# One 3x512-column VectorE transpose per block in place of three of 512 columns

## The chip, the cores and the metric

The program runs on one core of a Trainium2 chip. The metric is the device time of one execution in microseconds (us), as the median of several runs; lower is better. TensorE is called PE here, its weight loads PEld, VectorE DVE, ScalarE ACT, GpSimd POOL and SyncE SP, as in the profile.

## The reference

Eight sequences of 4096 tokens with 192 channels pass through a causal convolution of 7 taps, whose taps are a softmax shared by the 24 channels of a head, and then through a two-layer MLP with SiLU, 192 to 2048 to 192, all in float32:

```python
w = softmax(weight)                                  # 8 heads x 7 taps
x_pad = concatenate([zeros((B, 6, D)), x], axis=1)
out[b, s, h, g] = sum_k w[h, k] * x_unf[b, s, k, h, g]
x = out.reshape(B * S, D)                            # 32768 x 192
h = x @ w_in                                         # 192 x 2048
g = h * (1.0 / (1.0 + np.exp(-h)))
return (g @ w_out).astype(np.float32)                # 2048 x 192
```

## The kernel before

**Tiling.** The 32768 tokens are cut into 32 blocks of 1024 (`NB`), each block into two halves of 512 (`TB`). The 192 channels are three groups of 64 (`NK` = 3). In a tile of 128 partitions, partitions 0 to 63 hold 64 channels of the first half and 64 to 127 the same channels of the second.

**The input of a block.** `load` (L172) brings group k of a block from DRAM to `nat[:, k]` with four DMAs on SP's queue, 32 tokens to a partition in the order that leaves each 32x32 square still to be turned. `turn_in` (L462) turns group k with one VectorE stream transpose from `nat[:, k]` into `xt[:, k, 6:518]` (recorded at L465); the first 6 columns of `xt` are the halo. There is one `xt` tile for all blocks (`xts[b] = xts[0]`). `halo_in` (L477) then fills the halo: POOL copies the last 6 columns of the block before, and an SP DMA takes those of the first half to the second. `conv` (L490) makes the convolution of group k tap by tap, from `xt` back into `nat`: tap 0 on ACT, taps 1 to 6 on DVE (L499). `spread` (L506) copies the result by SP DMAs to the tile `dup`, and `win` makes sums and differences of it, so that both row halves of PE can read their operands.

**The MLP.** The first product is made in a form with fewer multiplications: for each of five groups g (handled in the order 0, 4, 1, 2, 3) `product` (L611) makes fifteen products r of a 64-row weight with a 64-row operand, in one row half of PE each (r in 0, 1, 2, 4, 5, 6, 11, 14 in rows 64 to 127, the others in rows 0 to 63). They add up in PSUM banks along three chains, and `sums_h` (L662) takes partial values out between two steps of a chain: `u` copies one to SBUF (ACT), `X` and `a` add a second chain to it, `b` subtracts the third chain (all DVE, recorded at L668), and `S` applies SiLU (ACT). The third chain of every group lies in bank 4, and `X4` writes bank 6, onto which product 11 then accumulates. The second product (`out_slot`, L741) uses the whole array in four column tiles; before it, `sum_g` (L709) makes differences of the SiLU outputs on DVE.

**The order.** Nothing in the steady part is left to a scheduler: `PLAN` (L81) is a list of tokens for one period, written out by hand, and `step` (L858) carries them out in that order for b = 3 and on (L1075); `START` (L107) is a longer list for the first three blocks. A token has a name and digits: `P12.2` is product 12 of group 2, `u2.3` output 2 of group 3; `+` sends it to the next block, `-` and `=` to the one or two before. An engine gets its instructions in the order of the tokens and carries them out in that order. `i.k` calls `turn_in` for the block after. In `PLAN` the three stand well apart, and each has work of its engine behind it:

```text
P3.4 -M7.0 S2.0 +i.2 u2.4 | P0.0 | P7.0 X2.4 | ... a5.0 ...
P7.1 a0.4 | P0.1 +i.1 u5.3 sp.1 | P12.1 a5.1 | ... -o.0 | P4.1 u2.2 b1.1 | ...
P11.1 -o.3 u0.2 | P13.2 S1.1 a0.1 | P6.3 S4.1 | P9.2 +i.0 | P0.2 b5.1 u2.3 +ha.0
| P3.3 S0.0 X4.2 | P1.3 S2.2 | P12.2 u1.2 | P11.2 X2.3 | P7.2 u0.3 b1.2 | ...
```

`ha.0` is `halo_in`. The tap-0 step of group 2, `+v.20`, comes eleven slots after `+ha.0`, and that of group 1 three slots later.

In `START` the third of the three tokens is `-i.2` for block 2, `i.2` for block 3 and `+i.1` for block 4. Block 0 is turned group by group ahead of everything, and block 1 by `i.0`, `i.1`, `i.2` in one go before the list begins. From block 5 to block 31, 27 blocks, the third token is the `+i.0` of `PLAN`.

Of the kernel before, what the change touches and what calls it, by code (L numbers as in the profile page):

```python
# [17 lines left out]
def kernel(  # L18
# [33 lines left out]
    NK = D // R  # L52
    grp = D // H
    pad = K - 1
    TB = 512
# [99 lines left out]
    def pin(ins):  # L155
        return tc.keep_in_program_order(ins)
# [13 lines left out]
    nats, xts, gs = {}, {}, {}  # L170
# [288 lines left out]

    tails = {}  # L460

    def turn_in(b, k):  # L462
        xts[b] = xts[0]
        pin(
            nc.vector.transpose(  # L465
                xts[b][:, k, pad : pad + TB], nats[b][:, k, :, :].rearrange("p k c -> p (k c)")
            )
        )
        if not b and k == NK - 1:
            tail_of(b)  # L470

    def tail_of(b):
        if (b + 1) * TT % S:
            tails[b + 1] = xpool.tile([R, NK, pad], F32, tag="tail", name="tail", bufs=2)
            pin(nc.sync.dma_start(out=tails[b + 1], in_=xts[b][R:P, :, TB : TB + pad]))
# [382 lines left out]
    def step(b, token):  # L858
# [19 lines left out]
        elif name[0] in "uXabS":  # L878
            sums_h(b, name, *digits)
        elif name == "t":  # L880
            sum_g(b, *digits)
        elif name[0] == "D":
            i, (j, e) = int(name[1]), digits
            for half in range(2) if i == 3 and b == NB - 1 else (None,):
                out_slot(b, j, i, e, half)
        elif name[0] in "Mzyx":
            merge(b, name, *digits)
        elif name == "o":
            turn_out(b, *digits)
        elif name == "st":  # L890
            store_out(b, *digits)
        elif name == "dp":
            next(downs)
        elif name == "cp":
            copy_plain(b, *digits)
        elif name == "go":
            pool.tensor_copy(warm, nats[1][:, digits[0], 0, 0:1])
            for g in (2, 3):
                for e in range(2):
                    combine(g, e)  # L900
        elif name == "ld":
            if b + 1 < NB:
                load(b + 1, digits)
        elif b + 1 < NB:
            {"i": turn_in, "ha": halo_in, "v": conv, "sp": spread, "w": win}[name](
                b + 1, *digits[: 1 + (name == "v")]
            )
# [97 lines left out]
    def conv_pe(k):  # L1005
        by_pe[k] = [bank() for _ in range(2)]
        for i in range(K):
            for n in range(2):
# [8 lines left out]
                )  # L1017

    turn_in(0, 0)

    vec.memset(xts[0][R:P, 1:NK, 0:pad], 0.0)
# [4 lines left out]
    round_in(0, 0)  # L1026
    diagonal(1)
    turn_in(0, 1)
    conv_pe(1)
    for j in (1, 2):  # L1030
# [80 lines left out]
```

## Time and profile before

| what | value |
|---|---|
| median of 3 runs | 2349.09 us (2348.8 to 2349.61) |
| the profiled execution's own time | 2349.19 us |
| its span in the profile | 2347.5 us |
| busy PE / DVE / ACT | 2340.3 / 2099.6 / 1187.3 us |
| input transposes (L465) | 96, 66.8 us busy, 698 ns mean |
| steady period, from one `i.2` to the next | 72.14 us (1121.67 to 1193.81 us) |

The span is what the profile covers of the 2349.19 us; 1.7 us lie around it. Starts and durations in the timeline are in us; the end of a matmul is modelled, so that consecutive matmuls overlap in the records, and the distance from start to start tells more than the busy time. Each product of `PLAN` shows as two matmuls of 512 columns in one row half of PE, 0.43 us from start to start; the two row halves run side by side. A wait that a product has is carried by its weight load, which is in the PEld rows.

### The profile page before, as it was taken

Reading aid. Unit: us, or ns where it says so; the run is one execution under the profiler, and the core shown is the slowest. Engines: PE = TensorE matmul, PEld = TensorE weight load, DVE = VectorE, ACT = ScalarE, POOL = GpSimd, SP = SyncE. Lnnn points to the kernel's source line nnn. Section 1 sums busy time; section 2 is a strip of 40 time slices with the busy share of each in tenths; the row PEclk is TensorE's granted clock in tenths of the full one; section 3 lists DMA queues with packets and bytes.
Section 4 is the critical chain, followed back from the end, with each engine's and each line's share of the span. In section 5 each row is a group of like instructions: output and inputs, shape, how many; then the busy total and the mean of one; then the engine's idle time right before and its main releaser. Section 6 shows DMA issues by size and latency. Waiting matters only on the chain.

```text
span 2347.5 us, 43988 instructions
## 1 busy us (share of the span) xinstructions
PE 2340.3 (100%) x17630; PEld 1061.0 (45%) x17630; DVE 2099.6 (89%) x2877; ACT 1187.3 (51%) x2275; POOL 96.8 (4%) x168
## 2 busy tenths in 40 slices
PE   9999999999999999999999999999999999999998
PEld 4344444444444444434444444444444444444445
DVE  8899989899899998998998999989999989899876
ACT  4345644456544466444564445654446644456443
POOL 4920000000000000000000000000000000000000
PEclk9999999999999999999999999999999999999999
DMA  7232212222121221222221222212222212222111
GB/s 158 52 66 48 47 27 47 38 53 53 29 41 36 53 53 31 39 43 46 53 49 31 42 38 53 53 29 42 36 53 53 38 33 45 43 53 44 20 24 25
DMA packets 451245, 106.56 MB, mean 45 GB/s; under 512 B 423584, under 2 KB 428704, under 8 KB 451040
## 3 DMA queue, kind: packets, MB, share of 16 engines
q1 hardware_dynamic: 447392, 101.78, 23.7%
q8 instruction: 138, 2.26, 0.4%
q0 software_dynamic: 448, 1.58, 0.3%
q10 hardware_dynamic: 3200, 0.39, 0.1%
q14 instruction: 67, 0.55, 0.1%
HBM read 31.46 MB, written 25.17 MB: 24 GB/s over the span
## 4 chain that ended last, share of the span: by engine, by line
PE 99%; DVE 0%; ACT 0%; issue 0%; ACTq 0%
PE ps L741 47%; PE ps L625 42%; PE ps L642 5%; PE ps L762 2%; PE ps L571 2%; PE ps L1010 1%; PE ps L423 0%; DVE t L709 0%; ACT g L686 0%; DVE cmb L163 0%; ACT u L163 0%; DVE osb L163 0%; DVE osb L829 0%; DVE g L668 0%; PE ps L449 0%
## 5 line engine op out<-in xcount | busy, mean ns | idle before, releaser
L625 PE MATMUL ps<-win,wr 64*128 64x512 f32 x1550 | 720.3, 597 | 0.0
L741 PE MATMUL ps<-g,wo 128*32 128x512 f32 x2976 | 702.4, 593 | 0.0
L625 PE MATMUL ps<-win,ws 64*128 64x512 f32 x1550 | 631.3, 595 | 0.0
L741 PE MATMUL ps<-t,wo 128*32 128x512 f32 (+2 forms) x4528 | 545.7, 446 | 0.0
L674 ACT COPY u<-ps 128x512 f32<-128x512 f32 x775 | 446.8, 586 | 173.6 <-PE ps L625 161.4
L741 PE MATMUL ps<-t,wx 128*32 128x512 f32 x2976 | 495.5, 592 | 0.1
L625 PE MATMUL ps<-dup,wr 64*128 64x512 f32 x868 | 425.4, 593 | 0.0
L499 DVE SCALAR_TENSOR_TENSOR nat<-xt,taps,nat 128x512 f32<-128x512 f32 x564 | 411.3, 753 | 3.8 <-ACT nat L496 3.6
L686 ACT ACTIVATE g<-g 128x512 f32<-128x512 f32 x465 | 286.1, 633 | 231.5 <-DVE g L668 231.5
L804 ACT COPY yx<-ps 32x512 f32<-32x512 f32 x150 | 86.9, 579 | 574.0 <-PE ps L741 572.3
L709 DVE TENSOR_TENSOR t<-g 128x1024 f32<-128x1024 f32 x248 | 300.6, 1219 | 51.1 <-PE ps L741 43.4
L625 PEld LDWEIGHTS ps<-win,wr 64*128 64x128 f32 x1550 | 275.6, 186 | 150.4 <-issue 67.8
L668 DVE TENSOR_TENSOR g<-u,ps 128x512 f32<-128x512 f32 x465 | 311.2, 680 | 28.8 <-PE ps L625 14.6
L625 PE MATMUL ps<-dup,ws 64*128 64x512 f32 x682 | 324.2, 599 | 0.0
L709 DVE TENSOR_TENSOR t<-g,t 128x1024 f32<-128x1024 f32 x248 | 301.8, 1217 | 12.2 <-PE ps L741 9.4
L741 PEld LDWEIGHTS ps<-t,wo 128*32 128x32 f32 x4528 | 186.7, 110 | 274.1 <-issue 247.6
L625 PEld LDWEIGHTS ps<-win,ws 64*128 64x128 f32 x1550 | 254.7, 186 | 110.5 <-issue 40.8
L686 ACT ACTIVATE g<-ps 128x512 f32<-128x512 f32 x465 | 266.8, 597 | 41.1 <-PE ps L625 38.4
L668 DVE TENSOR_TENSOR ps<-u,ps 128x512 f32<-128x512 f32 x310 | 214.7, 692 | 43.7 <-ACT g L686 19.0
L741 PE MATMUL ps<-g,wx 128*32 128x512 f32 x1488 | 250.5, 592 | 0.0
L741 PEld LDWEIGHTS ps<-g,wo 128*32 128x32 f32 x2976 | 170.2, 110 | 120.9 <-issue 118.9
L741 PEld LDWEIGHTS ps<-t,wx 128*32 128x32 f32 x2976 | 120.5, 110 | 217.5 <-issue 202.3
(90 smaller groups left out, 1764.5 us busy)
## 6 DMA issues: line engine op xcount, KB each, us to landing
dup<-nat SPq DMA_DIRECT2D x345, 128.0 KB, 2.3
nat<-in_x_dram SPq DMA_DIRECT2D x382, 64.0 KB, 2.4
out_dram<-osb SPq DMA_DIRECT2D x376, 64.0 KB, 2.0
raw<-in_moe_w_out_dram SPq DMA_DIRECT2D x8, 384.0 KB, 3.6
raw<-in_moe_w_in_dram SPq DMA_DIRECT2D x12, 192.0 KB, 4.7
ws<-wr POOLq DMA_DIRECT2D x8, 192.0 KB, 5.0
raw<-in_moe_w_in_dram SPq DMA_DIRECT2D x6, 128.0 KB, 3.1
xt<-xt SPq DMA_DIRECT2D x31, 4.5 KB, 1.9
```

The source lines that it names most:

```text
L499: nc.vector.scalar_tensor_tensor(out=dst, in0=src, scalar=tap, in1=dst, op0=ALU.mult, op1=ALU.add)
L571: nc.tensor.matmul(hs[a, n, e], rows(wr[j], e)[:, a, k, :], rows(d, e)[:, n, k, :], start=k == 0, stop=k == NK - 1,)
L625: nc.tensor.matmul(to[:, cols], raw(g, *LEFT[e][r], e), rhs[:, cols], start=first, stop=True, skip_group_check=True,)
L642: nc.tensor.matmul(banks[PLAIN_BANKS[n and 1 + e]][:, cols], rows(wr[j] if own == e else ws[j], e)[:, a, k, :], rows(dups[b], e)[:, SLOT[e ...
L668: pin(nc.vector.tensor_tensor(out_, u, v, op=op))
L674: pin(nc.scalar.copy(us[b, g, o][:, cols], t1[:, cols]))
L686: pin(nc.scalar.activation(h, src, AF.Silu))
L709: pin(nc.vector.tensor_tensor(t[i // 2][:, i % 2, :], u, v, op=ALU.subtract))
L741: nc.tensor.matmul(accs[b][at][SQ * q : SQ * q + SQ, to], lhs[:, e, SQ * k : SQ * k + SQ], rhs[:, e, ts(q, TB // 4) if i == 5 else to], st ...
L762: nc.tensor.matmul(banks[DOWN_BANKS[k]][R * n : R * n + R, :], wo[j][:, a, e, R * k : R * k + R], gs[b, j, a][:, n, e, :], start=j == 0 an ...
L804: pin(nc.scalar.copy(to, acc[3 * (name[0] == "x") + k][n:P, :]))
L1010: nc.tensor.matmul(by_pe[k][n], rows(diag, n)[:, k, i, :], rows(xts[0], n)[:, k, i : i + TB], start=i == 0, stop=i == K - 1,)
```

## The change

`turn_in` no longer turns a group when its token comes. For every block but the first it notes the token in a set, and when the third of the three has come it turns all three groups with one stream transpose of 3x512 columns, from `nat[:, 0:3]` to `xt[:, 0:3, 6:518]`. The first two tokens of a block issue nothing. In the steady period the one operation stands where `+i.0` stood. Block 0 is turned group by group as before. Neither list of tokens is touched.

```diff
@@ -459,14 +459,21 @@
     tails = {}
 
+    turned = {}
+
     def turn_in(b, k):
         xts[b] = xts[0]
+        done = turned.setdefault(b, set())
+        done.add(k)
+        if b and len(done) < NK:
+            return
+        k = slice(0, NK) if b else slice(k, k + 1)
         pin(
             nc.vector.transpose(
-                xts[b][:, k, pad : pad + TB], nats[b][:, k, :, :].rearrange("p k c -> p (k c)")
-            )
-        )
-        if not b and k == NK - 1:
+                xts[b][:, k, pad : pad + TB], nats[b][:, k, :, :].rearrange("p k q c -> p k (q c)")
+            )
+        )
+        if not b and len(done) == NK:
             tail_of(b)
```

## The prediction, made before the changed kernel was run

> **What bounds the kernel.** I read the page first: busy shares, and the chain that ended last.
>
> ```profile
> PE 2340.3 (100%) x17630; PEld 1061.0 (45%) x17630; DVE 2099.6 (89%) x2877; ACT 1187.3 (51%) x2275; POOL 96.8 (4%) x168
> ...
> PE 99%; DVE 0%; ACT 0%; issue 0%; ACTq 0%
> ```
>
> PE is the bound throughout; DVE is idle a tenth of the time. So work taken off DVE is worth nothing in itself, and what counts is whether PE waits for DVE somewhere. The table of waits, for PE's weight loads, says that it does:
>
> ```profile
> PEld ps L625 <- DVE ps L668: 57.8, 214, 0.8
> ...
> PEld ps L625 <- DVE g L668: 24.1, 71, 0.8
> ```
>
> These hundreds of waits are short, and most are hidden behind the matmul in progress, but they show DVE's sums running just ahead of the products. There an operation that is three times as long matters by its place. Next come the prices of transposes, in the groups of DVE by shape (busy us, mean ns):
>
> ```profile
> L829 DVE STREAM_TRANSPOSE osb<-cmb 96x512 f32<-96x512 f32 x120 | 83.8, 698 | 0.0
> L465 DVE STREAM_TRANSPOSE xt<-nat 128x512 f32<-128x512 f32 x96 | 66.8, 698 | 0.7 <-DMA nat<-in_x_dram 0.7
> ...
> L163 DVE STREAM_TRANSPOSE osb<-cmb 96x256 f32<-96x256 f32 x4 | 1.7, 433 | 0.1
> ...
> L163 DVE STREAM_TRANSPOSE osb<-cmb 96x512 f32<-96x512 f32 x2 | 1.4, 704 | 0.0
> ```
>
> 256 columns more cost 271 ns, so 1.06 ns a column over a fixed part of some 0.16 us. Then the place of `i.0` in a steady period, in the timeline of DVE (start, duration):
>
> ```profile
> 1137.91 0.70 DVE L668 TENSOR_TENSOR ps<-u,ps 128x512 f32<-128x512 f32 x1 [0.47 <-ACT g L686]
> 1138.52 0.70 DVE L829 STREAM_TRANSPOSE osb<-cmb 96x512 f32<-96x512 f32 x1
> 1139.14 0.65 DVE L668 TENSOR_TENSOR g<-u,ps 128x512 f32<-128x512 f32 x1
> 1139.72 0.69 DVE L465 STREAM_TRANSPOSE xt<-nat 128x512 f32<-128x512 f32 x1
> 1140.34 0.65 DVE L668 TENSOR_TENSOR g<-g,ps 128x512 f32<-128x512 f32 x1
> 1140.91 0.68 DVE L668 TENSOR_TENSOR ps<-u,ps 128x512 f32<-128x512 f32 x1
> ```
>
> By the tokens these are `X2.2`, `o.3`, `a0.1`, `i.0`, `b5.1` and `X4.2`, back to back after `X2.2`, which waited for ACT. The weight loads, and then the matmuls, that depend on the last two:
>
> ```profile
> 1141.04 0.18 PEld L625 LDWEIGHTS ps<-win,wr 64*128 64x128 f32 x1
> ...
> 1141.64 0.30 PEld L625 LDWEIGHTS ps<-dup,wr 64*128 64x128 f32 x2
> ...
> 1144.97 0.18 PEld L625 LDWEIGHTS ps<-win,wr 64*128 64x128 f32 x1 [0.45 <-DVE ps L668]
> ```
>
> ```profile
> 1141.38 0.59 PE L625 MATMUL ps<-win,wr 64*128 64x512 f32 x1
> 1141.75 0.59 PE L625 MATMUL ps<-dup,wr 64*128 64x512 f32 x1
> ...
> 1144.97 0.69 PE L625 MATMUL ps<-win,wr 64*128 64x512 f32 x1
> ```
>
> 1141.04 is `P12.2`, first in bank 4, which `b5.1` has just read: `b5.1` ends at 1140.98, the load goes 0.05 later. 1141.64 is `P11.2`, which accumulates onto what `X4.2` wrote: end 1141.59, load 0.05 later. Their matmuls follow at 1141.38 and 1141.75. So the slack is about 0.34 us for `P12.2` and 0.11 for `P11.2`. The third pair, `P7.3`, shows the price of arriving late: the load is no longer covered, the matmul lasts 0.69 and not 0.59, so about 0.10 more. The true slack is 0.24 and none. For `i.2` I looked at its place too:
>
> ```profile
> 1121.67 0.70 DVE L465 STREAM_TRANSPOSE xt<-nat 128x512 f32<-128x512 f32 x1
> 1121.69 0.58 ACT L674 COPY u<-ps 128x512 f32<-128x512 f32 x1
> ...
> 1122.31 0.70 DVE L668 TENSOR_TENSOR ps<-u,ps 128x512 f32<-128x512 f32 x1
> ```
>
> `X2.4` follows `u2.4`, which ends at 1122.27: `i.2` fills a hole that ACT makes.
>
> [...]
>
> **The change part by part.**
>
> 1. The operation. No row has 1536 columns. From the slope: 0.70 + 1024 x 1.06 ns = 1.78 us. From above: three of 0.70, 2.09, if nothing of the fixed part is saved. [...] I take 1.78. DVE does 0.31 us less a block.
>
> 2. `i.2` and `i.1` go. `i.2`: nothing, `X2.4` is still held by ACT to 1122.3. `i.1` (1134.19): `a5.1`, `o.0` and `b1.1` come up to 0.6 earlier, but PE's row halves step at 0.43 us without a stall from there to 1140.8, and `X2.2` is held to 1137.91 by an ACT activation that itself waited for PE. Nothing. These covers are the work of ACT and PE; without them a gain of up to 0.6 a place would be possible.
>
> 3. `i.0` grows. `X2.2` fixes its start at 1139.72. Everything behind it in DVE's queue moves by 1024 x 1.06 ns = 1.08 us. `b5.1` then runs 1141.42 to 1142.07, the load of `P12.2` goes at 1142.12, its second matmul 0.53 later at 1142.65 instead of 1141.81: **0.84 us late** in the lower row half. `X4.2` runs 1141.99 to 1142.67, `P11.2` loads at 1142.72, its second matmul at 1143.25 instead of 1142.18: **1.07 late** in the upper half. Both chains then go on at 0.43 a step, as before; later loops (`P9.3`, `X4.3`, `P7.3`) start from products equally late, so they keep their waits. The row halves meet at the first `out_slot` of the period (1150.31). The lower half's last matmul starts at 1149.79, the upper's at 1149.52, so the upper has 0.27 to spare: 1.07 - 0.27 is under 0.84. So 0.84 a period. ACT, back to back from 1144.52 to there, waits for upper-half products and comes 1.07 late; its SiLU outputs feed `out_slot`, and if they bind it is 1.07 a period.
>
> 4. What is moved past. The operation waits for the loads of all three groups; those of group 0 are last, and `i.0` waited for them already. The SP queue holds the halo DMA behind it (issued at 1140.47), then the tail, six stores and the next loads to about 1147.3: all 1.07 later, with PE itself 0.84 later, and SP is then waiting for later work. The first readers of `xt` on ACT (`+v.20` at 1145.00) are late as well, with over 2 us since the halo was issued. I cost these at nothing; SP's and ACT's own slack covers them.
>
> 5. `START` and block 1. Block 1's three were adjacent and gain 0.3 us of DVE, under PE's work: 0. Block 2's third lies where DVE then idles 2.8 us for the halo: 0. Block 3's (149.15) has the `i.2` of 147.41 taken from ahead of it: 1.08 - 0.63 - 0.07 idle, up to 0.3. Block 4's (203.65) is in back-to-back sums, both row halves late behind them: 1.1. Together 1.3.
>
> Sum: 27 x 0.84 + 1.3 = 24.0 us. On the profiled execution's own 2349.19 this gives 2373.2; it is within 0.1 of the median, so 2373.
>
> **Rivals.**
>
> - *The upper half or ACT sets the end*: 27 x 1.07 + 1.3 = 30.2, 2379. For: ACT has no gap there. Against: the 0.27 us above.
> - *The operation costs three full prices, 2.09 us*: 1.39 longer, less 0.24 is 1.15; 27 x 1.15 + 2.0 = 33, 2382. Against: the slope.
> - *PE takes part of it back*: the lower half has 0.16 + 0.10 us lost at `P7.3` and 0.09 ahead of `out_slot`; if all of it closed, 0.49 a period, 14.5 us, 2364. Against: these waits follow the late products.
> - *Not slower*: [...] no cost in the period, 2350. The freed slots could then close the waits on DVE ahead of `i.0` (late loads at 1130.70 and 1133.55, some 0.25 each): up to 0.5 x 27 = 13.5 faster, 2336. It decides below about 0.94 us. Against: the slope, and both these waits lie behind the hole at `i.2`.
> - *The change doesn't do what it says*: each of blocks 1 to 31 has its three tokens in the lists, so a merged operation should come once for each. Otherwise 2349; 1 in 100.
>
> **How the numbers follow.** 0.84 a period 45 in 100, the upper half or ACT 20, full prices 12, partly taken back 13, no cost 5 (the last rival with it), faster 5. Within 0.2% (4.7 us) is about what a measurement here can tell from no change. Slower: 0.45 + 0.20 + 0.12 + 0.13 = 0.90. The range goes from 2361, just under the part taken back, to 2383, just over full prices.
>
> **What would show it.** 34 transposes at L465 (3 + 31), the long ones at 1.78 us; `b5.1` 1.7 us after the start of the long one; the loads of `P12.2` and `P11.2` with a wait on DVE near 1 us; the steady period 73.0 us, the stretch from `i.0` to the first `out_slot` longer by 0.84 and all others unchanged; DVE busy about 10 us less. The prediction is wrong if the operation is under 0.94 or over 2.1 us, if DVE reaches `i.0` earlier, or if PE's delay closes by 1150.

## The result, and the profile after

The changed kernel takes 2373.15 us (median of 4 runs, 2372.92 to 2373.3) against 2349.35 us (4 runs, 2348.8 to 2349.8): 1.0102 times as long, 95% interval 1.009 to 1.0114. The prediction was 2373. The profiled execution took 2373.12 us, its span is 2371.3 us.

The page of the changed kernel, busy shares and the chain that ended last; lines of the code have moved by 7:

```profile
PE 2357.8 (99%) x17630; PEld 1071.4 (45%) x17630; DVE 2098.7 (89%) x2815; ACT 1186.0 (50%) x2275; POOL 96.8 (4%) x168
...
PE 93%; DVE 4%; issue 1%; ACT 1%; DVEq 0%; ACTq 0%
```

The chain was 99% PE and is now 93%: DVE has 4% of it. PE does the same matmuls, so the time is not work but waiting. Its busy time grows by 17.5 us all the same (2340.3 to 2357.8): it counts the time in which any record is open, and while one row half waits, records of the other, with their modelled ends, cover most of the wait (at `P12.2`, below, only 0.19 us shows as idle). The durations of the matmuls added up have not grown (9724 us before, 9723 after). The operation itself, in the groups of DVE by shape (busy us, mean ns):

```profile
L472 DVE STREAM_TRANSPOSE xt<-nat 128x1536 f32<-128x1536 f32 x31 | 54.6, 1760 | 0.0
```

It is issued once for each of 31 blocks and takes 1.76 us. The steady period, from one of them to the next, is 72.97 us (1078.02 to 1150.99) instead of 72.14. Its place in the period that corresponds to the one shown of the kernel before, on DVE's timeline (start, duration). PE runs 11.28 us later by then, the delay of the periods before, so 11.28 is to be taken off each time to compare:

```profile
1149.18 0.70 DVE L675 TENSOR_TENSOR ps<-u,ps 128x512 f32<-128x512 f32 x1 [0.50 <-ACT g L693]
1149.79 0.70 DVE L836 STREAM_TRANSPOSE osb<-cmb 96x512 f32<-96x512 f32 x1
1150.41 0.64 DVE L675 TENSOR_TENSOR g<-u,ps 128x512 f32<-128x512 f32 x1
1150.99 1.76 DVE L472 STREAM_TRANSPOSE xt<-nat 128x1536 f32<-128x1536 f32 x1
1152.67 0.65 DVE L675 TENSOR_TENSOR g<-g,ps 128x512 f32<-128x512 f32 x1
1153.24 1.28 DVE L675 TENSOR_TENSOR ps<-u,ps 128x512 f32<-128x512 f32 x2
```

The sum behind (`b5.1`) starts 1.68 us after the long transpose and not 0.62. What PE's weight loads make of it:

```profile
1153.37 0.29 PEld L632 LDWEIGHTS ps<-win,wr 64*128 64x128 f32 x2 [1.01 <-DVE g L675]
1153.98 0.18 PEld L632 LDWEIGHTS ps<-dup,wr 64*128 64x128 f32 x1 [0.32 <-DVE ps L675]
```

These are `P12.2` and `P11.2`. Without 11.28 they lie at 1142.09 and 1142.70, where they were at 1141.04 and 1141.64. Their matmuls, `P12.2` as both in one row and then the second of `P11.2`:

```profile
1153.37 1.12 PE L632 MATMUL ps<-win,wr 64*128 64x512 f32 x2 [0.19 <-DVE g L675]
...
1154.52 0.59 PE L632 MATMUL ps<-dup,wr 64*128 64x512 f32 x1
```

The second of `P12.2` starts 0.53 after the first, at 1153.90. Without 11.28 the two seconds are at 1142.62 and 1143.24, where they were at 1141.81 and 1142.18: the lower row half is some 0.82 late and the upper 1.06. And the end of the stage, the last products and the first `out_slot`, on PE's timeline:

```profile
1161.76 0.59 PE L632 MATMUL ps<-dup,wr 64*128 64x512 f32 x1
1161.89 0.59 PE L632 MATMUL ps<-win,wr 64*128 64x512 f32 x1
1162.41 0.64 PE L748 MATMUL ps<-g,wo 128*32 128x512 f32 x4
```

Without 11.28 the `out_slot` starts at 1151.13 instead of 1150.31, 0.82 later; by the lengths of the periods it is 0.83. From there to the next transpose every matmul keeps that delay; nothing is given back and nothing added.

The freed places earn nothing. Where `i.2` stood, DVE now idles ahead of `X2.4`:

```profile
1133.58 0.70 DVE L675 TENSOR_TENSOR ps<-u,ps 128x512 f32<-128x512 f32 x1 [0.56 <-ACT u L681]
...
1145.98 0.69 DVE L675 TENSOR_TENSOR g<-u,ps 128x512 f32<-128x512 f32 x1 [0.43 <-PE ps L632]
```

The second line is `a5.1`, behind the former `i.1`: it waits for PE.

### The profile page after: what moved, and what is told of

Same layout as the page of the kernel before. It is cut to its first block, busy times and chain, and to the rows that moved or that the text cites. A ratio compares the mean times of both kernels' runs of the same rounds, so it can differ in the third digit from the quotient of the medians.

```text
span 2371.3 us, 43892 instructions
## 1 busy us (share of the span) xinstructions
PE 2357.8 (99%) x17630; PEld 1071.4 (45%) x17630; DVE 2098.7 (89%) x2815; ACT 1186.0 (50%) x2275; POOL 96.8 (4%) x168
## 4 chain that ended last, share of the span: by engine, by line
PE 93%; DVE 4%; issue 1%; ACT 1%; DVEq 0%; ACTq 0%
PE ps L748 47%; PE ps L632 37%; PE ps L649 5%; PE ps L769 2%; PE ps L578 2%; DVE g L675 2%; DVE xt L472 1%; ACT g L693 1%; DVE ps L675 1%; DVE osb L836 1%; PE ps L1017 1%; PE ps L423 0%; DVE t L716 0%; DVE nat L506 0%; DVE cmb L163 0%
## 5 line engine op out<-in xcount | busy, mean ns | idle before, releaser
L632 PE MATMUL ps<-win,wr 64*128 64x512 f32 x1550 | 727.7, 599 | 5.4 <-DVE g L675 5.4
L632 PE MATMUL ps<-dup,ws 64*128 64x512 f32 x682 | 330.7, 598 | 0.0
L632 PEld LDWEIGHTS ps<-win,ws 64*128 64x128 f32 x1550 | 261.0, 186 | 113.3 <-issue 36.0
```

What stands on the lines that cost most here:

```text
L632: nc.tensor.matmul(to[:, cols], raw(g, *LEFT[e][r], e), rhs[:, cols], start=first, stop=True, skip_group_check=True,)
```

## The experiments

The theory under test: each period costs the time by which the sums behind the transposes are held back at that one place, less a slack of 0.24 us, that of the lower row half. The rivals are that the long operation as such is slow, that the loss is in proportion to the columns, that the figure is a loss net of a gain at the freed places, and that the upper row half sets the end. The time of the kernel before is 2348.99 us (16 runs) beside the first four and 2349.24 us (25 runs) beside the last three. The edits are to `turn_in` of the changed kernel; `turn(s)` stands for its transpose of the groups in `s`.

**Three where the one stood.**

```diff
-        k = slice(0, NK) if b else slice(k, k + 1)
-        turn(k)
+        for i in range(NK) if b else (k,):
+            turn(slice(i, i + 1))
```

> Three transposes of 512 columns stand one behind the other where the one of 3x512 stood. Theory (what counts is the time DVE is held at that place, less 0.24 us of slack of the lower row half): each goes 0.62 us after the one before, so the sums behind come 1.24 us later than in the kernel before, PE 1.00 us a period; 27 x 1.00 + 1 = 28 us, about 2377.5, slower than the changed kernel by 4 to 5 us. Rival (the long operation itself is the trouble, not the place): 2349 to 2360, well under the changed kernel's 2373.

Measured: 2376.68 us, ratio 1.0117 (1.01 to 1.0134), steady period 73.09 us. DVE's timeline and the load of `P12.2`:

```profile
1737.62 1.88 DVE L471 STREAM_TRANSPOSE xt<-nat 128x512 f32<-128x512 f32 x3
1739.42 0.64 DVE L679 TENSOR_TENSOR g<-g,ps 128x512 f32<-128x512 f32 x1
```

```profile
1740.12 0.29 PEld L636 LDWEIGHTS ps<-win,wr 64*128 64x128 f32 x2 [1.13 <-DVE g L679]
```

The sum comes 1.80 us after the first transpose, 1.18 later than the 0.62 before; the period is 0.95 longer, 0.23 less. In the trace the second transpose starts 0.62 us after the first, but the third and the sum each 0.59 after the one before, where 0.62 each was expected: so it is 0.95 and not 1.00, and the run is 3.5 us over the changed kernel and not 4 to 5. The long operation as such is not the trouble: it is cheaper than three at the same place.

**The first two kept, and the long one.**

```diff
-        if b and len(done) < NK:
-            return
-        turn(slice(0, NK) if b else slice(k, k + 1))
+        last = b and len(done) == NK
+        turn(slice(0, NK) if last else slice(k, k + 1))
```

> The first two transposes of a block stand as before, and the third is the one of 3x512 columns, which turns the two others again. Theory: the places that the change frees earn nothing, so it takes what the changed kernel takes, 2373 (2372 to 2375), with 1.2 us more DVE work in each period. Rival (the 0.83 us a period are a larger loss net of a gain at the freed places): slower than 2373 by that gain, up to 2386.

Measured: 2372.83 us, ratio 1.0101 (1.0086 to 1.0116), period 72.97 us. Its page:

```profile
PE 2357.8 (99%) x17630; PEld 1074.1 (45%) x17630; DVE 2131.8 (90%) x2877; ACT 1184.9 (50%) x2275; POOL 96.7 (4%) x168
```

DVE is busy 33 us more than in the changed kernel, PE exactly as long, and the time is the same. The freed places are worth nothing.

**Two of three at the last place.**

```diff
-        if b and len(done) < NK:
-            return
-        turn(slice(0, NK) if b else slice(k, k + 1))
+        if b < 5 or k == 2:
+            turn(slice(k, k + 1))
+        elif k == 0:
+            turn(slice(0, 2))
```

> From block 5 on, group 2 is turned at its own place, and groups 0 and 1 by one operation of 2x512 columns at the place of the last. Theory: 0.53 us more at that place, less 0.24 of slack, so 0.29 us a period and 7.8 in all: 2357. Rival (loss in proportion to the columns added, half of the changed kernel's): 0.42 us a period, 2360.5. Rival (the upper row half sets the end): no slack, 0.53 a period, 2363.5.

Measured: 2357.25 us, ratio 1.0035 (1.0021 to 1.0048), period 72.44 us, 0.30 over the kernel before. DVE's timeline:

```profile
1939.85 1.22 DVE L471 STREAM_TRANSPOSE xt<-nat 128x1024 f32<-128x1024 f32 x1
1941.00 0.65 DVE L679 TENSOR_TENSOR g<-g,ps 128x512 f32<-128x512 f32 x1
```

The sum comes 1.15 us behind, 0.53 later; less 0.30 is 0.23 again. The rivals had 0.42 and 0.53 a period.

**A short one more, under the slack.** Every group is turned at its own place, as in the kernel before, and:

```diff
+        if b > 4 and k == 0:
+            pin(
+                nc.vector.transpose(
+                    xts[b][:, 1, pad : pad + 4 * SQ],
+                    nats[b][:, 1, 0:4, :].rearrange("p q c -> p (q c)"),
+                )
+            )
```

> The kernel before, with one more transpose from block 5 on, of 128 columns of group 1 (turned again), right behind that of group 0. It holds DVE some 0.22 us more at that place. Theory: under the slack of 0.24 us, so nothing: 2349.4, at most 1 us over. Rival (loss in proportion to the time added): 0.17 us a period, 2354.

Measured: 2349.3 us, ratio 1.0001 (0.9993 to 1.001), period 72.14 us. DVE's timeline, and the weight loads:

```profile
2005.45 0.69 DVE L471 STREAM_TRANSPOSE xt<-nat 128x512 f32<-128x512 f32 x1
2006.07 0.27 DVE L479 STREAM_TRANSPOSE xt<-nat 128x128 f32<-128x128 f32 x1
2006.27 0.64 DVE L683 TENSOR_TENSOR g<-g,ps 128x512 f32<-128x512 f32 x1
```

```profile
2006.96 0.34 PEld L640 LDWEIGHTS ps<-win,wr 64*128 64x128 f32 x2
2007.58 0.18 PEld L640 LDWEIGHTS ps<-dup,wr 64*128 64x128 f32 x1 [0.27 <-DVE ps L683]
```

The sums come 0.19 us later and the load of `P11.2` now waits, but the period is unchanged. Two slacks swallow it: the lower half has its 0.24, and the upper half, which runs 0.19 late from `P11.2` on, has its 0.27 ahead of the first `out_slot`, where the delay is gone. A loss in proportion would have been 4 to 5 us.

**Two of three at the middle place.**

```diff
-        if b and len(done) < NK:
-            return
-        turn(slice(0, NK) if b else slice(k, k + 1))
+        if b < 5 or k == 0:
+            turn(slice(k, k + 1))
+        elif k == 1:
+            turn(slice(1, 3))
```

> From block 5 on, groups 2 and 1 are turned by one operation of 2x512 columns at the place of i.1, and group 0 at its own. Theory by the same reading at another place: a5.1 and b1.1 come 0.53 us later; the load of P4.1 has 0.04 us of true slack (upper row half, 0.49 late, of which 0.27 is spare at the end), that of P10.1 has 0.28 (lower half, 0.25 late): 0.25 us a period, 6.8 in all, 2356. Rival (only the place of i.0 is tight): 2349.4.

Measured: 2357.07 us, ratio 1.0033 (1.0021 to 1.0046), period 72.40 us, 0.26 over. The place in the kernel before, where `i.1` starts at 1134.19: the loads of `P4.1` and `P10.1`.

```profile
1135.52 0.33 PEld L625 LDWEIGHTS ps<-win,ws 64*128 64x128 f32 x2
...
1136.70 0.18 PEld L625 LDWEIGHTS ps<-dup,ws 64*128 64x128 f32 x1
```

In this run, DVE and then the same loads:

```profile
1934.60 1.24 DVE L471 STREAM_TRANSPOSE xt<-nat 128x1024 f32<-128x1024 f32 x1
1935.76 0.65 DVE L679 TENSOR_TENSOR g<-u,ps 128x512 f32<-128x512 f32 x1
```

```profile
1936.46 0.18 PEld L636 LDWEIGHTS ps<-win,ws 64*128 64x128 f32 x1 [0.50 <-DVE g L679]
...
1937.65 0.29 PEld L636 LDWEIGHTS ps<-dup,ws 64*128 64x128 f32 x2
```

Counted from the start of the transpose, the loads come 0.53 and 0.54 us later. Set against the trace of the kernel before, matmul by matmul, `P4.1` and what follows it in the upper half run 0.50 us late and `P10.1` and what follows in the lower half 0.26, and 0.26 is what the period keeps. So the place of `i.0` is not the only tight one; the same reading gives the price of another.

**No transposes at all.**

```diff
-        if b and len(done) < NK:
-            return
-        turn(slice(0, NK) if b else slice(k, k + 1))
+        if b < 5:
+            turn(slice(k, k + 1))
```

> From block 5 on no block's input is turned at all; what the convolution reads there is left from block 4. Theory: in the kernel before the three transposes lie in slack, so leaving them out earns next to nothing: 2349.4, no more than 2 us under. Rival (PE waits for DVE wherever it is busy, so that 1.9 us of DVE work a period is worth something): up to 0.5 us a period, 2336.

Measured: 2349.64 us, ratio 1.0002 (0.9993 to 1.001), period 72.14 us. Its page:

```profile
PE 2340.0 (100%) x17630; PEld 1057.9 (45%) x17630; DVE 2058.2 (88%) x2796; ACT 1188.5 (51%) x2275; POOL 96.9 (4%) x168
```

With 81 transposes fewer than the kernel before the time is the same. In that kernel the three lie in slack altogether, so another arrangement of them has nothing to win from PE's waiting.

**The first blocks alone.**

```diff
-        if b and len(done) < NK:
-            return
-        turn(slice(0, NK) if b else slice(k, k + 1))
+        if not b or b > 4:
+            turn(slice(k, k + 1))
+        elif len(done) == NK:
+            turn(slice(0, NK))
```

> Blocks 1 to 4 are turned by one operation each, all others as before. Theory: the prediction had 1.3 us for these, the changed kernel's trace shows PE 0.97 us late after them: 2350.3. If the blocks of the first stretch carried more of the loss than that: over 2351.

Measured: 2350.54 us, ratio 1.0006 (0.9997 to 1.0015). The medians are 1.30 us apart, within the interval of no change, but the trace is sharper: PE is 0.09 us late ahead of block 4's transposes and 1.06 behind them, so that place costs 0.97. The rest of the 1.4 us by which its span is longer is one delay of 0.33 near 2070 us, far from these blocks.

Together, for the place of `i.0` (all in us; the first is the delay of the sums behind it, by start of the transposes to start of `b5.1`, less 0.62):

| kernel | delay | longer period | difference |
|---|---|---|---|
| 128 columns more | 0.19 | 0.00 | (0.19) |
| two at the last place | 0.53 | 0.30 | 0.23 |
| the change | 1.07 | 0.83 | 0.24 |
| three in a row | 1.18 | 0.95 | 0.23 |

## Why the prediction was right

By its steps:

- *The bound.* PE it was; the time came from PE waiting, as the chain of the changed kernel shows.
- *1, the operation.* 1.78 us was said by the slope, 1.76 measured. From 512 to 1536 columns (698 to 1760 ns) that is 1.04 ns a column over a fixed part of some 0.17 us, an estimate from these two means; three operations of 698 ns come to 2.09 us. The rival of no cost in the period, which needed an operation under about 0.94 us, is out, and so is that of full prices.
- *2, the freed places.* Nothing, shown by the run that kept both and by the one without any.
- *3, the growth of `i.0`.* The sums were to come 1.08 late, and came 1.07. The second matmul of `P12.2` was to be 0.84 late and that of `P11.2` 1.07; the trace has 0.82 and 1.06. The lower half sets the end: its last product starts at 1161.89, the upper's at 1161.76. The upper half has 0.13 us to spare there where the sum said 0.04 (0.84 - 1.07 + 0.27). The sum let it stay 1.07 late to the end. But its last product, the `P5.0` at the head of the next period's list, waits for an ACT activation before and after: its load is at 1148.98 and at 1161.23, 0.97 later. ACT has made up 0.10 of its 1.07 by then, which the prediction did not see. ACT did not bind: the load of the second `out_slot`, which waits for it in both traces, goes from 1150.77 to 1162.87, as late as the first.
- *4, what it is moved past.* No cost: the whole of the period's growth is there at the first `out_slot`, and nothing is added behind.
- *5, the first blocks.* 1.3 was the sum (its terms, 0.3 and 1.1, make 1.4), 0.97 the measurement: block 3's place cost nothing, block 4's 0.97. The first steady period made up for it with 1.18 instead of 0.84: near 268.4 us one sum (`X2.1`) started 0.35 us later than in other periods. Its cause is open, and it is not shown to be the change's: the run that kept the first two transposes has no such delay there, and single ones of that size stand elsewhere, 0.35 near 345 us in the run without transposes, 0.33 near 2070 in that of the first blocks, 0.34 near 2290 in that of 128 columns more. That it brought the total to within 0.3 of the forecast is luck; without it the forecast would have been some 0.6 too high.
- *The total.* 0.97 + 1.18 + 26 x 0.83 = 23.7 us, against 2371.3 - 2347.5 = 23.8 of the spans. From one period to the next PE's delay grows by 0.80 to 0.87 us, but for that first step and one of 1.00.
- *A rival half right?* That PE takes part of it back: no. The weight load of `P7.3` is at 1157.07; without 11.28 that is 0.82 later than the 1144.97 of before, as late as the products ahead of it, as the prediction had argued. The wait that it shows is 0.22 us and was 0.45, but only because it is counted from the load before, one of the upper half, which is later still.

Two of its signs were off. DVE's busy time was to fall by about 10 us and fell by 0.9. The transposes alone did lose 10 us (66.8 to 54.6 + 2.1), but busy time is the union of the records, and records back to back overlap by some 0.08 us (`o.3`: 0.70 long, the next start 0.62 behind). All durations of DVE added up fell by 9.2 us, but their overlaps fell by 8.2: 62 records are gone, and some of the others now stand after a wait and count in full. And only the load of `P12.2` shows a wait near 1 us; that of `P11.2` shows 0.32, since its wait is counted from the load before it.

## What to carry to other kernels

DVE is not the bound here, and its transposes were priced by place: 512 columns more cost 0.30 us a period at one place and 0.26 at another, and 81 transposes left out earned nothing. To read such a price, take the time by which the work behind is held up. For each consumer on the bounding engine take off its slack: the gap from its weight load to its matmul, less what an uncovered load costs (0.10 us here), and what its path has to spare where the paths meet again (0.27 us for the upper half here). What is left on the worst path is the price; with the measured delays it came out within 0.02 us at the two places where it was tried. A merge that saves 0.3 us of DVE's work was a loss here, because it turned three places of 0.6 us into one stop of 1.7. Whether a place has slack to give can be measured cheaply by leaving the work out, or by adding a short piece to it.

## What the runs showed beyond that

By the means of the records, a float32 stream transpose took 265 ns for 128 columns, 433 for 256 (on 96 partitions, the others on 128), 698 for 512, 1224 to 1238 for 1024 and 1760 for 1536. In the run of three in a row, the second of 512 columns started 0.62 us after the first, and the third and the addition 0.59 us after the one before.

Set against the trace of the kernel before, PE falls back in six of the eight other profiled executions, once or twice in each, by some 0.3 us more in one period than in its neighbours (0.29 to 0.35). So a price is to be read from several periods and not from one.
